# Gated linear attention: the first eight loads re-cut, re-ordered and issued from two engines

## The chip, the cores and the metric

One of the eight cores of a Trainium2 chip runs the whole kernel. The metric is the device time of one execution in microseconds. The kernel before was run three times.

## What is computed

Eight batches of linear attention with eight heads, 576 tokens and 64 channels a head, and behind it a gated block over 512 channels. Cut to what matters:

```
q_s = exp(q - max over the 64 channels);  q_s /= sum over the 64 channels + 1e-9
k_s = exp(k - max over the 576 tokens);   k_s /= sum over the 576 tokens + 1e-9
kv  = einsum('bhsd,bhse->bhde', k_s, v)
x   = einsum('bhsd,bhde->bhse', q_s, kv)          # then heads side by side: 512 channels
gate_pre[s] = sum over 5 taps of conv_w[tap] * x[s - 4 + tap]
gate = 1 / (1 + exp(-gate_pre))
out  = (gate * (x @ w_val)) @ w_out
```

q, k and v are float32. The two weight matrices and the convolution's taps are 64-bit floats; they reach the core as pairs of 32-bit words, and the core makes float32 numbers of them.

## The kernel before, in words

The tokens of a batch lie on the partitions in four chunks of 128 and a tail of 64; the tails of two batches share one tile. For batches 0 and 1 the keys come with the channels on the partitions, as four blocks of 128 channels by 576 tokens; later batches take another way, which the change does not touch.

There is no loop nest that sets the order. `ORDER` (line 32) is a list of some thousand steps written out by hand; the last lines of the kernel call the function of each step in that order. Every engine takes its instructions in this order, one after the other, and waits at the first one whose data are not there. So the place of a step among the others is the kernel's schedule.

The steps at the start that this text speaks of, with their lines:

- `load_q b c0 c1` (206) loads the chunks c0 to c1 of a batch's q; with c1 = 5 on an even batch the tail comes too, as a transfer of its own. `load_kc b p` (314) loads a block of keys, `load_words i` (225) a slab of weight words (0 to 3 of w_val, 4 to 7 of w_out), `load_ident` (233) the identity matrix that TensorE's transposes use. All of them are issued on SyncE (SP). The framework gives each transfer one of eight completion semaphores in turn, and a transfer that takes a semaphore again waits on SP until the transfer that had it before has landed. So at most eight transfers are under way, and SP's queue stands still while it waits.
- A weight slab becomes float32 by `part` (238, ScalarE here), `field` (244), `scaled` (250) and `signed` (254, VectorE, two instructions) and `joined` (260, GpSimd), which needs both sides. `w_high` (269) rounds it into the first of two weight tiles.
- Of q, `q_max` (357, VectorE) takes the negative maximum per head. Chunk 2 of batch 0 goes through `q_each` (381), eight ScalarE exponentials with the maximum as their bias; the other chunks through `q_sub` (363, GpSimd) and `q_exp` (368, ScalarE). `q_sum` (372) and `q_mul` (387) divide by the sum.
- Of a block of keys, `k_top` (318, VectorE) takes the negative maximum and `k_raise` (324, ScalarE) the exponential; `k_turn` (328) transposes on TensorE and `k_turned` (335) copies back.

Line 588 loads the table of the exponential on ScalarE before any step; the four memsets behind it run on GpSimd.

Of the kernel before, what the change touches and what calls it, by code (L numbers as in the profile page):

```python
# [11 lines left out]
AF = mybir.ActivationFunctionType  # L12
# [7 lines left out]
NB = C // P  # L20
# [9 lines left out]


ORDER = [step.strip() for step in """
    load_words 3, load_q 0 2 5, load_kc 0 2, load_kc 0 0, load_q 0 1 2, load_kc 0 3, load_kc 0 1, load_words 0, field 3,
    part 3 a, scaled 3 v, signed 3, joined 3, load_ident, q_max 0 2 3, load_words 1, q_max 0 3 5, q_each 0 2,
    w_high 3 p, load_q 0 0 1, k_top 0 2, q_sub 0 4 p, load_q 1 0 5, k_top 0 0, k_raise 0 2, load_kc 1 3, q_sub 0 3 p,
    q_max 0 1 2, k_raise 0 0, load_kc 1 0, k_top 0 3, q_sub 0 1 p, q_exp 0 4 5, load_v 0, k_top 0 1, k_raise 0 3,
    load_vt 0, part 0 a, field 0, k_turn 0 1, load_words 2, scaled 0 v, q_exp 0 3 4, signed 0, k_raise 0 1, load_kc 1 2,
# [109 lines left out]
def gated_linear_attention(ctx: ExitStack, tc: tile.TileContext, q, k, v, qt, kt, vt, kc, km, w_val, w_out, ident_in, out):  # L147
    nc = tc.nc
# [11 lines left out]
    def block(tag, name, bufs, dtype=F32, n=S):  # L160
        return work.tile([P, S], dtype, tag=tag, name=name, bufs=bufs)[:, :n]

    def pair(name, dtype, tag="pair", bufs=6):
        return work.tile([P, 2 * S], dtype, tag=tag, name=name, bufs=bufs)
# [18 lines left out]
    T = {}  # L183
# [4 lines left out]
    def cols(h):  # L188
        return {"a": slice(0, C), "l": slice(0, C // 2), "r": slice(C // 2, C)}[h]
# [6 lines left out]
    def load_k(b, h="a"):  # L196
        if ("k", b) not in T:
            T["k", b] = big.tile([P, 4, C], F32, tag="k", name=f"k{b}")
        nc.sync.dma_start(out=T["k", b][:, :, cols(h)], in_=k[b, :, :, cols(h)])

    def load_kt(b):
        if b % 2 == 0:
            T["kt", b] = T["kt", b + 1] = big.tile([P, C], F32, tag="kt", name=f"kt{b}", bufs=1)
            nc.sync.dma_start(out=T["kt", b], in_=kt[b // 2])

    def load_q(b, c0=0, c1=5):
        if ("q", b) not in T:
            T["q", b] = big.tile([P, 5, C], F32, tag="q", name=f"q{b}")
        nc.sync.dma_start(out=T["q", b][:, c0:min(c1, 4)], in_=q[b, :, c0:min(c1, 4)])
        if c1 == 5 and b % 2 == 0:  # L210
            nc.sync.dma_start(out=T["q", b][:, 4], in_=qt[b // 2])

    def load_v(b):
        T["v", b] = big.tile([P, 4, H, D + 1], F32, tag="v", name=f"v{b}")
# [7 lines left out]
    def slab(i):  # L222
        return slice(P * (i % NB), P * (i % NB) + P)

    def load_words(i):

        n = C + TAPS * (i < NB)
        place = ("under", 2) if i in (4, 5) else ("pair", 6)
        t = pair(f"words{i}", I32, *place)[:, :2 * n]
        T["words", i] = t.rearrange("p (n t) -> p n t", t=2)  # L230
        nc.sync.dma_start(out=t, in_=(w_val, w_out)[i // NB][i % NB])

    def load_ident():
        nc.sync.dma_start(out=ident, in_=ident_in)

# [73 lines left out]

    def load_kc(b, p):
        t = T["kc", b, p] = block(("gh", "gl")[b], f"kc_{b}_{p}", 4)
        nc.sync.dma_start(out=t, in_=kc[b, p])

    def k_top(b, p):
        if ("ktop", b) not in T:
# [260 lines left out]
    ident = const.tile([P, P], F32, tag="ident", name="ident")  # L580
# [4 lines left out]
    ]  # L585
    kvd = [const.tile([P, NB, P], F32, tag=f"kvd{i}", name=f"kvd{i}") for i in range(2)]
    ktz = [const.tile([P, C], F32, tag=f"ktz{i}", name=f"ktz{i}") for i in range(2)]
    nc.scalar.preload_act_table(AF.Exp)
    for t in kvd + ktz:
        nc.gpsimd.memset(t, 0.0)  # L590

# [51 lines left out]
```

## Time and profile before

| | us |
|---|---|
| three runs | 304.69, 305.14, 306.5 (median 305.14) |
| profiled execution | 305.72 |
| span of its instructions | 303.9 |

| engine | busy us | share of the span |
|---|---|---|
| TensorE (PE) | 279.1 | 92% |
| its weight loads (PEld) | 271.1 | 89% |
| VectorE (DVE) | 255.5 | 84% |
| ScalarE (ACT) | 216.2 | 71% |
| GpSimd (POOL) | 220.4 | 73% |

The profiled execution is 1.8 us longer than the span, which runs from the first instruction to the last; a sum made within the span is carried to the execution's time by adding these 1.8 us. The share of an engine is a mean over the whole span. At the start TensorE has nothing to do yet, and the other engines and the transfers decide; there the timeline (start, duration, engine, line, what is written from what, and in brackets the idle time before it with what ended it) and the chain of waits say more than the shares. SPq stands for SP's queue of transfers: its rows are the issues, not the transfers.

### The profile page before, as it was taken

The numbers are of one execution on the slowest core, as the hardware profiler recorded it, in microseconds if no ns is written. First come the engines' busy times: TensorE is split into PE (matmuls) and PEld (weight loads), VectorE is DVE, ScalarE is ACT, GpSimd is POOL, SyncE is SP. The second block draws the span as 40 slices with busy tenths as digits, with TensorE's granted clock in tenths as the row PEclk, the third lists the DMA queues.
The fourth block names the chain that finished last, engine by engine and source line by source line (L and its number), as shares of the span: only waits on it lengthen the run. The fifth ranks groups of instructions, "written<-read, shape, count | busy, mean of one in ns | idle before, by whom it ended". The sixth has DMA issues, their size and how long they took to land.

```text
span 303.9 us, 6467 instructions
## 1 busy us (share of the span) xinstructions
PE 279.1 (92%) x2536; PEld 271.1 (89%) x2536; DVE 255.5 (84%) x350; ACT 216.2 (71%) x357; POOL 220.4 (73%) x206
## 2 busy tenths in 40 slices
PE   0347899999999899999999999999999999999995
PEld 0336699999989799999999999999998999999995
DVE  3999999999999798999999898999779876836611
ACT  3999999967795996869673964659496885464220
POOL 4677959799989699659787879784886949752500
PEclk9978999999999999999999999999999999999999
DMA  7999491389598822618597099023201210021012
GB/s 240 408 405 396 156 397 45 103 187 361 194 319 261 327 102 75 217 54 284 158 395 304 39 259 332 17 90 106 38 0 39 80 41 0 2 116 41 0 62 96
DMA packets 17454, 51.25 MB, mean 169 GB/s; under 512 B 2705, under 2 KB 3089, under 8 KB 14737
## 3 DMA queue, kind: packets, MB, share of 16 engines
q1 hardware_dynamic: 17424, 50.85, 47.9%
q8 instruction: 20, 0.33, 0.5%
q14 instruction: 10, 0.07, 0.1%
HBM read 41.39 MB, written 9.45 MB: 167 GB/s over the span
## 4 chain that ended last, share of the span: by engine, by line
PE 66%; ACT 11%; DVE 10%; DMA 7%; issue 2%; POOL 2%; SPq 1%; ACTq 0%; DVEq 0%
PE out L534 26%; PE val L534 25%; PE x L487 7%; PE kv L407 4%; PE qTps L439 3%; DVE qs L377 3%; DMA q<-in_q 3%; DMA words<-in_w_val 2%; ACT q L392 2%; DMA out<-o 2%; DVE qm L361 1%; ACT L523 1%; DVE qs L378 1%; ACT qT L171 1%; DVE gate L511 1%
## 5 line engine op out<-in xcount | busy, mean ns | idle before, releaser
L534 PE MATMUL val<-x,w_val_hi 128*128 128x288 f32 x512 | 88.4, 294 | 0.0
L534 PEld LDWEIGHTS val<-x,w_val_hi 128*128 128x128 f32 x512 | 74.8, 188 | 0.0
L511 DVE SCALAR_TENSOR_TENSOR gate<-x,cw,gate 128x573 f32<-128x573 f32 (+3 forms) x91 | 72.1, 807 | 2.2 <-ACT gate L500 1.2
L520 POOL TENSOR_TENSOR gate<-gate,far 128x572 f32<-128x572 f32 (+3 forms) x37 | 49.5, 1341 | 27.3 <-ACT far L516 26.4
L534 PE MATMUL out<-gh,w_out_lo 128*128 128x288 f32 x256 | 55.9, 297 | 1.1 <-ACT o L171 0.6
L534 PE MATMUL val<-x,w_val_lo 128*128 128x288 f32 x256 | 56.0, 299 | 0.0
L534 PE MATMUL out<-gh,w_out_hi 128*128 128x288 f32 x256 | 55.0, 294 | 0.0
L534 PEld LDWEIGHTS out<-gh,w_out_lo 128*128 128x128 f32 x256 | 41.2, 188 | 2.1 <-ACT o L171 0.9
L534 PEld LDWEIGHTS val<-x,w_val_lo 128*128 128x128 f32 x256 | 40.7, 188 | 0.7 <-DVE x L173 0.2
L534 PEld LDWEIGHTS out<-gh,w_out_hi 128*128 128x128 f32 x256 | 41.2, 188 | 0.0
L560 POOL TENSOR_TENSOR gl<-g,gh 128x576 fp32r<-128x576 f32 x24 | 34.6, 1449 | 7.2 <-ACT gh L171 5.0
L534 PE MATMUL out<-gl,w_out_hi 128*128 128x288 f32 x256 | 39.2, 294 | 0.0
L516 ACT ACTIVATE far<-x,cw 128x572 f32<-128x572 f32 (+3 forms) x37 | 27.0, 745 | 13.7 <-DVE gate L511 6.7
L534 PEld LDWEIGHTS out<-gl,w_out_hi 128*128 128x128 f32 x256 | 35.7, 188 | 0.0
L552 DVE TENSOR_TENSOR g<-val,gate 128x576 f32<-128x576 f32 x32 | 24.0, 751 | 10.0 <-PE val L534 5.8
L366 POOL TENSOR_TENSOR q<-q,qm 128x512 f32<-128x512 f32 x29 | 31.0, 1086 | 0.7 <-issue 0.7
L171 ACT COPY o<-out 128x576 f32<-128x576 f32 x27 | 17.2, 637 | 16.7 <-PE out L534 11.5
L301 POOL TENSOR_TENSOR k<-k,kmax 128x512 f32<-128x512 f32 x21 | 28.6, 1377 | 0.1
L506 DVE TENSOR_TENSOR x<-x,x 128x576 fp32r<-128x576 f32 x32 | 23.2, 747 | 6.3 <-ACT far L516 4.1
L523 ACT ACTIVATE gate<-gate 128x576 f32<-128x576 f32 x32 | 21.1, 685 | 8.4 <-DVE gate L511 5.4
L394 POOL TENSOR_TENSOR q<-q,qs 128x512 f32<-128x512 f32 x25 | 26.0, 1048 | 0.8 <-DVE qs L379 0.6
L500 ACT ACTIVATE gate<-x,cw 128x576 f32<-128x576 f32 x27 | 19.9, 747 | 6.8 <-PE x L487 5.2
(88 smaller groups left out, 522.1 us busy)
## 6 DMA issues: line engine op xcount, KB each, us to landing
out<-o SPq DMA_DIRECT2D x31, 288.0 KB, 2.2
v<-in_v SPq DMA_DIRECT2D x8, 1040.0 KB, 8.9
q<-in_q SPq DMA_DIRECT2D x7, 1024.0 KB, 7.7
km<-in_k_strided SPq DMA_DIRECT2D x24, 288.0 KB, 4.8
k<-in_k SPq DMA_DIRECT2D x6, 1024.0 KB, 7.9
kc<-in_k_channels SPq DMA_DIRECT2D x8, 288.0 KB, 7.6
words<-in_w_val SPq DMA_DIRECT2D x4, 517.0 KB, 6.9
words<-in_w_out SPq DMA_DIRECT2D x4, 512.0 KB, 7.7
```

The source lines that it names most:

```text
L301: engine(e).tensor_sub(kk[r, cs], kk[r, cs], mx[r, cs])
L366: engine(e).tensor_tensor(qq, qq, m, op=ALU.add if b < 2 else ALU.subtract)
L394: engine(e).tensor_mul(qq, qq, s.unsqueeze(2).broadcast_to([P, H, D]))
L487: nc.tensor.matmul(T["x", b, p][:, cs], a, z[:, cs], start=(i == 0), stop=(i == len(parts) - 1))
L506: nc.vector.tensor_sub(xl, T["x", b, p], T["xh", b, p].bitcast(F32))
L511: nc.vector.scalar_tensor_tensor(out=a, in0=x, scalar=w, in1=a, op0=ALU.mult, op1=ALU.add)
L516: nc.scalar.activation(T["far", b, p, j], T["x", b, p][:, :S - n], AF.Copy, scale=cw[:, p, j:j + 1])
L520: nc.gpsimd.tensor_add(a, a, T["far", b, p, j])
L523: nc.scalar.activation(T["gate", b, p], T["gate", b, p], AF.Sigmoid)
L534: nc.tensor.matmul(ps[:, cs], a[:, kb, ms], z[:, cs], start=(i == 0), stop=(i == len(parts) - 1))
L552: nc.vector.tensor_mul(T["g", b, m], T["val", b, m], T["gate", b, m])
L560: engine(e).tensor_sub(T["gl", b, m], T["g", b, m], T["gh", b, m].bitcast(F32))
```

## The change

It touches the first rows of `ORDER` and the functions behind them.

- q of batch 0 was loaded as chunks 2 and 3 in one transfer of 512 KB and the tail as a second; now chunk 2 alone (256 KB) is the first transfer of SP, then chunk 3, then the tail.
- Weight slab 3 (517 KB), the first transfer before, and key block 2 of batch 0 (288 KB) are issued by ScalarE.
- The table of the exponential is loaded by a step of its own, `table`, behind these two issues on ScalarE.
- `q_max 0 2 3` and `q_each 0 2` stand ahead of weight slab 3's steps; `q_max 0 3 5` keeps its place behind them.

```diff
 ORDER = [step.strip() for step in """
-    load_words 3, load_q 0 2 5, load_kc 0 2, load_kc 0 0, load_q 0 1 2, load_kc 0 3, load_kc 0 1, load_words 0, field 3,
-    part 3 a, scaled 3 v, signed 3, joined 3, load_ident, q_max 0 2 3, load_words 1, q_max 0 3 5, q_each 0 2,
+    load_q 0 2 3, load_words 3 a, load_q 0 3 5, load_kc 0 2 a, table, load_kc 0 0, load_q 0 1 2, load_kc 0 3, load_kc 0 1,
+    load_words 0, q_max 0 2 3, q_each 0 2, field 3, part 3 a, scaled 3 v, signed 3, joined 3, load_ident, load_words 1, q_max 0 3 5,
     w_high 3 p, load_q 0 0 1, k_top 0 2, q_sub 0 4 p, load_q 1 0 5, k_top 0 0, k_raise 0 2, load_kc 1 3, q_sub 0 3 p,
...
+    def queue(e):
+        return {"s": nc.sync, "a": nc.scalar}[e]
+
+    def table():
+        nc.scalar.preload_act_table(AF.Exp)
+
...
-    def load_q(b, c0=0, c1=5):
+    def load_q(b, c0=0, c1=5, e="s"):
...
-        nc.sync.dma_start(out=T["q", b][:, c0:min(c1, 4)], in_=q[b, :, c0:min(c1, 4)])
+        queue(e).dma_start(out=T["q", b][:, c0:min(c1, 4)], in_=q[b, :, c0:min(c1, 4)])
...
-        nc.sync.dma_start(out=t, in_=(w_val, w_out)[i // NB][i % NB])
+        queue(e).dma_start(out=t, in_=(w_val, w_out)[i // NB][i % NB])
...
-        nc.sync.dma_start(out=t, in_=kc[b, p])
+        queue(e).dma_start(out=t, in_=kc[b, p])
...
-    nc.scalar.preload_act_table(AF.Exp)
```

How the order moves is shown for three engines. A row has the line, the instruction, what is written from what (words3 is weight slab 3, kc_0_2 key block 2 of batch 0, q0 and qm_0 batch 0's q and its maxima, ktop_0 the maxima of the keys, e3 and f3 the two halves of a slab under work; the last number is a buffer's) and in brackets the semaphores that it waits for; DMAHW0 to DMAHW7 are the eight of the transfers.

SP's queue at the start of the program, before:

```order
L231 DMA words3_89<-in_w_val 128x1034
L209 DMA q0_91<-in_q 128x1024
L211 DMA q0_91<-in_q_tail 128x512
L316 DMA kc_0_2_94<-in_k_channels 128x576
L316 DMA kc_0_0_96<-in_k_channels 128x576
L209 DMA q0_91<-in_q 128x512
L316 DMA kc_0_3_99<-in_k_channels 128x576
L316 DMA kc_0_1_101<-in_k_channels 128x576
L231 DMA words0_103<-in_w_val 128x1034 [waits DMAHW0_49]
L234 DMA ident_72<-in_ident 128x128 [waits DMAHW1_49]
```

And with the change:

```order
L215 DMA q0_88<-in_q 128x512 x2
L217 DMA q0_88<-in_q_tail 128x512
L322 DMA kc_0_0_97<-in_k_channels 128x576
L215 DMA q0_88<-in_q 128x512
L322 DMA kc_0_3_100<-in_k_channels 128x576
L322 DMA kc_0_1_102<-in_k_channels 128x576 [waits DMAHW0_49]
L237 DMA words0_104<-in_w_val 128x1034 [waits DMAHW1_49]
L240 DMA ident_72<-in_ident 128x128 [waits DMAHW2_49]
```

Two rows have left SP, and one transfer has become two. There are now nine transfers ahead of weight slab 0, so key block 1 is the first that waits for a semaphore (that of slab 3, DMAHW0); slab 0 waits for q's chunk 2 (DMAHW1) where it waited for slab 3.

ScalarE at the start, before:

```order
L588 ACT_TABLE_LOAD
L177 ACTIVATE f3_107<-words3_89 128x517 [waits DMAHW0_49]
L385 ACTIVATE q0_91<-q0_91,qm_0_114 128x64 [waits DMAHW1_49,DVE_49]
L385 ACTIVATE q0_91<-q0_91,qm_0_114 128x64 x7
L326 ACTIVATE kc_0_2_94<-kc_0_2_94,ktop_0_129 128x576 [waits DMAHW3_49,DVE_49]
```

And with the change:

```order
L237 DMA words3_90<-in_w_val 128x1034
L322 DMA kc_0_2_94<-in_k_channels 128x576
L205 ACT_TABLE_LOAD
L391 ACTIVATE q0_88<-q0_88,qm_0_106 128x64 [waits DMAHW1_49,DVE_49]
L391 ACTIVATE q0_88<-q0_88,qm_0_106 128x64 x7
L177 ACTIVATE f3_118<-words3_90 128x517 [waits DMAHW0_49]
L332 ACTIVATE kc_0_2_94<-kc_0_2_94,ktop_0_130 128x576 [waits DMAHW2_49,DVE_49]
```

Two issues stand ahead of the table's load, and the eight exponentials of chunk 2 have passed ahead of slab 3's `part`.

VectorE at the start, before:

```order
L248 TENSOR_SCALAR e3_105<-words3_89 128x517 [waits DMAHW0_49]
L181 TENSOR_SCALAR e3_105<-e3_105 128x517 [waits DVE_49]
L257 TENSOR_SCALAR e3_105<-e3_105 128x517 [waits DVE_49]
L258 SCALAR_TENSOR_TENSOR e3_105<-words3_89,e3_105 128x517 [waits DVE_49]
L361 TENSOR_REDUCE qm_0_114<-q0_91 128x8 [waits DMAHW1_49]
L361 TENSOR_REDUCE qm_0_114<-q0_91 128x16 [waits DMAHW2_49]
```

And with the change:

```order
L367 TENSOR_REDUCE qm_0_106<-q0_88 128x8 [waits DMAHW1_49]
L254 TENSOR_SCALAR e3_116<-words3_90 128x517 [waits DMAHW0_49]
L181 TENSOR_SCALAR e3_116<-e3_116 128x517 [waits DVE_49]
L263 TENSOR_SCALAR e3_116<-e3_116 128x517 [waits DVE_49]
L264 SCALAR_TENSOR_TENSOR e3_116<-words3_90,e3_116 128x517 [waits DVE_49]
L367 TENSOR_REDUCE qm_0_106<-q0_88 128x16 [waits DMAHW4_49,DMAHW3_49]
```

The maximum of chunk 2 has moved from the fifth place to the first. All that follows on VectorE, and all of GpSimd's and TensorE's rows, keep their order.

More of the change, by code (lines that the diff above doesn't have):

```diff
@@ L204, in load_kt @@
             nc.sync.dma_start(out=T["kt", b], in_=kt[b // 2])
-    def load_q(b, c0=0, c1=5):
+    def load_q(b, c0=0, c1=5, e="s"):
         if ("q", b) not in T:
             T["q", b] = big.tile([P, 5, C], F32, tag="q", name=f"q{b}")
-        nc.sync.dma_start(out=T["q", b][:, c0:min(c1, 4)], in_=q[b, :, c0:min(c1, 4)])
+        queue(e).dma_start(out=T["q", b][:, c0:min(c1, 4)], in_=q[b, :, c0:min(c1, 4)])
         if c1 == 5 and b % 2 == 0:
-            nc.sync.dma_start(out=T["q", b][:, 4], in_=qt[b // 2])
+            queue(e).dma_start(out=T["q", b][:, 4], in_=qt[b // 2])
     def load_v(b):
@@ L223, in slab, with load_words @@
         return slice(P * (i % NB), P * (i % NB) + P)
-    def load_words(i):
+    def load_words(i, e="s"):
         n = C + TAPS * (i < NB)
@@ L230, in load_words, with load_ident @@
         T["words", i] = t.rearrange("p (n t) -> p n t", t=2)
-        nc.sync.dma_start(out=t, in_=(w_val, w_out)[i // NB][i % NB])
-    def load_ident():
-        nc.sync.dma_start(out=ident, in_=ident_in)
+        queue(e).dma_start(out=t, in_=(w_val, w_out)[i // NB][i % NB])
+    def load_ident(e="s"):
+        queue(e).dma_start(out=ident, in_=ident_in)
     def part(i, e="a"):
@@ L309, in kt_exp, with load_kc @@
         nc.scalar.activation(ktz[b % 2][r, cs], T["kt", b][r, cs], AF.Exp)
-    def load_kc(b, p):
+    def load_kc(b, p, e="s"):
         t = T["kc", b, p] = block(("gh", "gl")[b], f"kc_{b}_{p}", 4)
-        nc.sync.dma_start(out=t, in_=kc[b, p])
+        queue(e).dma_start(out=t, in_=kc[b, p])
     def k_top(b, p):
```

## The prediction

> **What bounds the kernel now.** I read the chain of waits first, because it tells which stretch the change can reach. Its columns are start, duration and what the end of the kernel hung on.
>
> ```profile
> 4.90 7.30 DMA words<-in_w_val
> 12.20 0.02 issue
> 12.23 0.44 DVE e L248
> ...
> 27.38 0.62 DVE ktop L322
> 28.00 0.02 issue
> 28.03 0.77 ACT kc L326
> 28.80 1.21 ACT qT L171 x2
> 30.01 0.04 issue
> 30.06 1.24 PE x L487 x4
> ```
>
> The start hangs on one transfer, weight slab 0, which lands at 12.20. Then VectorE works without a break to 28.00, ScalarE to 30.06, and from there the chain is mostly TensorE (66% of the span in the page's shares). The change acts ahead of 12.23 only; what it wins or loses there reaches the end only if VectorE and ScalarE carry it to 30.06. So I read the busy times by stretch next (busy time and count of each engine, then TensorE's granted clock, the transfer engines' busy share and GB/s).
>
> ```profile
> 0.00:12.20 12.20, 0.00 (x0) 0.00 (x0) 7.10 (x11) 6.60 (x14) 7.00 (x13) 1.00 0.86 304
> 12.20:28.00 15.80, 10.65 (x115) 9.56 (x116) 15.43 (x27) 15.12 (x39) 11.74 (x13) 0.78 1.03 403
> 1.66:5.07 3.41, 0.00 (x0) 0.00 (x0) 0.65 (x2) 1.03 (x2) 0.98 (x3) 1.00 0.94 269
> 5.07:8.48 3.41, 0.00 (x0) 0.00 (x0) 3.27 (x6) 1.31 (x6) 1.78 (x2) 1.00 1.00 371
> ```
>
> From 12.20 to 28.00 VectorE is busy 15.43 of 15.80 us and ScalarE 15.12: both are full, and the rest is ScalarE's wait for VectorE shown below. Ahead of it VectorE is busy 7.10 us and mostly waits for its first data. The transfer engines are busy from early on but move 269 and then 371 GB/s, against 403 later. VectorE's timeline has these waits in brackets:
>
> ```profile
> 4.38 0.43 DVE L248 TENSOR_SCALAR e<-words 128x517 f32<-128x517 f32 x1 [4.38 <-DMA words<-in_w_val]
> ...
> 6.45 1.98 DVE L361 TENSOR_REDUCE qm<-q 128x8 f32<-128x512 f32 x2
> 8.35 1.40 DVE L322 TENSOR_REDUCE ktop<-kc 128x1 f32<-128x576 f32 x2
> 9.67 0.68 DVE L361 TENSOR_REDUCE qm<-q 128x8 f32<-128x512 f32 x1
> 10.26 1.40 DVE L322 TENSOR_REDUCE ktop<-kc 128x1 f32<-128x576 f32 x2
> ...
> 12.23 0.43 DVE L248 TENSOR_SCALAR e<-words 128x517 f32<-128x517 f32 x1 [0.56 <-DMA words<-in_w_val]
> ```
>
> It starts at 4.38, when slab 3 has landed, works to 11.66 (10.26 + 1.40) and stands 0.56 us until slab 0 is there. So two things set 12.23: VectorE's queue, with 0.56 us to spare, and the landing of slab 0. A gain needs both.
>
> **The change, part by part.** When do the first two transfers land now? SP's rows before (issue, duration), its wait, and one small transfer from later on:
>
> ```profile
> 0.74 0.38 SPq L231 DMA_DIRECT2D words<-in_w_val  x1
> ...
> 4.90 0.47 SPq L231 DMA_DIRECT2D words<-in_w_val  x1
> 6.45 0.33 SPq L234 DMA_DIRECT2D ident<-in_ident  x1
> ...
> SPq L234 <- DMA q<-in_q: 1.1, 1, 1.1
> ...
> km<-in_k_strided SPq DMA_DIRECT2D x1, 288.0 KB, 2.8
> ```
>
> Slab 3's 517 KB, issued at 0.74, were there at 4.38. The identity's issue waited for q's chunks 2 and 3, so these 512 KB landed by 6.45: 2.07 us behind, 253 GB/s. With the change chunk 2 (256 KB) and slab 3 are issued side by side at about 0.74.
>
> - Chunk 2's landing, L2. Lower bound: had it the engines for itself, the km row's 2.8 us for 288 KB gives 0.74 + 2.8 = 3.5. Upper bound: both land together, after 773 KB at the old rate, 4.38 + 2.07 / 2 = 5.4. I take equal shares by bytes: chunk 2 is there when about 512 KB have come, 4.4.
> - Slab 3's landing, L3: from 4.4 (unchanged) to 5.4 (behind all 773 KB). I take 5.0, 5.4 less the gain of the next point.
> - Slab 0's landing. The bytes ahead of it are the same; only the slow ramp can shrink, by a gain g. Lower bound 0: the transfer engines' share is already 0.94 in the stretch from 1.66. Upper bound: at 403 GB/s the 512 KB would take 1.30 us in place of 2.07 (0.77 won); the km row leaves 2.8 - 0.73 = 2.07 us for what doesn't move bytes, and slab 3's bytes need 1.31 at 403, so 3.38 in place of 3.64 (0.26 won). Together 1.0. I take 0.4, nearer to 0 because of the 0.94: slab 0 can be used at 12.23 - 0.40 = 11.83.
>
> VectorE. Its work ahead of slab 0 is the same 7.28 us (4.38 to 11.66), of which chunk 2's maximum is 0.68, the like of the row at 9.67. Now the maximum goes first: its queue is through at the later of L2 + 0.02 + 7.28 = 11.70 and L3 + 0.02 + 6.60 = 11.62. That is ahead of 11.83, so slab 0 decides: -0.40. The cover is 0.13 us; the bounds of L2 and L3 give 11.0 to 12.7.
>
> ScalarE and GpSimd. Chunk 2's exponentials, now ahead of slab 3's `part`, hold up GpSimd's `joined`, and what it does for q:
>
> ```profile
> 0.73 1.28 ACT L588 ACT_TABLE_LOAD   x1 [0.73 <-PEq L632]
> 4.38 0.68 ACT L177 ACTIVATE f<-words 128x517 int32<-128x517 uint32 x1 [2.37 <-DMA words<-in_w_val]
> 7.17 2.02 ACT L385 ACTIVATE q<-q,qm 128x64 f32<-128x64 f32 x8 [2.11 <-DVE qm L361]
> 9.13 1.44 ACT L326 ACTIVATE kc<-kc,ktop 128x576 f32<-128x576 f32 x2
> 10.47 0.61 ACT L370 ACTIVATE q<-q 128x512 f32<-128x512 f32 x1
> 11.04 0.78 ACT L326 ACTIVATE kc<-kc,ktop 128x576 f32<-128x576 f32 x1
> 12.23 0.69 ACT L177 ACTIVATE f<-words 128x517 int32<-128x517 uint32 x1 [0.41 <-DMA words<-in_w_val]
> ...
> 6.64 1.28 POOL L261 TENSOR_TENSOR f<-e,f 128x517 int32<-128x517 int32 x1 [4.00 <-DVE e L258]
> 7.98 0.61 POOL L173 CAST w_val_hi<-f 128x512 fp32r<-128x512 f32 x1
> 8.55 3.04 POOL L366 TENSOR_TENSOR q<-q,qm 128x512 f32<-128x512 f32 x3
> ```
>
> From L2: the maximum 0.72 with its hops, the eight exponentials 1.96 (7.17 to 9.13), `part` 0.68, a hop of 0.1, `joined` 1.34 (6.64 to 7.98), the cast 0.57 (7.98 to 8.55), the first subtraction 1.04 (3.04 is three, overlapping), its exponential 0.6, a key block 0.65 to 0.7, so 7.66 us to slab 0's `part`, the row at 12.23. With L2 = 4.4 that is 12.06, behind slab 0 (11.83) but ahead of the old 12.23. ScalarE is then 0.23 us later than VectorE would like, and has this to spare:
>
> ```profile
> ACT kc L326 <- DVE ktop L322: 0.7, 1, 0.7
> ```
>
> 0.7 us of waiting for VectorE just ahead of 28.03. So the delay on ScalarE costs nothing; without that cover it would cost 0.23. The table's load (1.28) moves behind two issues of at most 0.5 each and ends by 3.0, while ScalarE waits for chunk 2's maximum until about 5.1; uncovered, at most 1.28. SP has one issue fewer, but key block 1 now waits for slab 3 and slab 0's issue moves from 4.90 to about 5.5. It took 7.30 us from issue to landing there, most of it in the queue, so 0.6 us later costs nothing; if the queue ran dry it would be 0.6. GpSimd, 1.3 us later up to 12.8, is ready before slab 0's `joined` needs it (14.47 less 0.4). Each later transfer still waits for the one eight places ahead, so all landings move with the ramp.
>
> The sum: -0.40 at 12.23, carried by VectorE's queue to 28.00 and by ScalarE to TensorE's start, 29.66 in place of 30.06; from there nothing is changed. The profiled 305.72 becomes 305.3; it stands 0.58 above the median of the runs, so against 305.14 I forecast 304.7.
>
> **The rivals.**
>
> *The ramp doesn't shrink* (0.27): g = 0, slab 0 lands at 12.20 as before, and VectorE's head start only lengthens its 0.56 us wait: 305.1. For it speaks the share of 0.94; against it that these busy engines moved 269 GB/s, time in which a second queue may get bytes through. The Trainium skill ("DMA: Bandwidth & Descriptors", "Issuing engines are not separate DMA queues") says that transfers started by different engines run on the same 16 DMA engines and interleave, and that issuing from several only saves the sequencer's time; by that rule this rival is the result. No run here yet has a second queue.
>
> *The full ramp* (0.17): chunk 2 by 3.5, slab 3 by 4.4, g = 1.0. VectorE is through at 11.0, ScalarE at 11.2, slab 0 usable at 11.23: -1.0, so 304.1. Against it: the first bytes cost more than 2 us whatever the queue.
>
> *The first data come later* (0.11, the slower side): L2 = L3 = 5.4. VectorE is through at 12.7, +0.5, and ScalarE at 13.1, +0.85, of which its 0.7 us cover all but 0.15: VectorE decides, 305.6. It decides from L2 = 4.93 on (4.93 + 0.02 + 7.28 = 12.23), only 0.5 above what I take.
>
> *ScalarE's queue is served behind SP's* (0.03): slab 3 would come behind the six transfers that SP has issued by 3.5, with the last key blocks, near 10.1 (they are used from 10.26 on): 10.1 + 6.6 = 16.7, +4.5, 309.6. Nothing in a trace with one queue excludes it.
>
> *The clock* (0.04). The rows of five stretches:
>
> ```profile
> 15.31:18.72 3.41, 0.93 (x8) 0.69 (x7) 3.34 (x6) 3.41 (x8) 3.27 (x4) 1.00 1.03 409
> ...
> 22.14:25.55 3.41, 3.41 (x69) 3.41 (x67) 3.34 (x8) 3.41 (x10) 3.06 (x4) 0.50 1.06 418
> 25.55:28.96 3.41, 2.24 (x25) 1.63 (x22) 3.27 (x8) 2.73 (x7) 3.07 (x4) 1.00 0.99 381
> 28.96:32.38 3.42, 2.88 (x20) 2.38 (x21) 3.34 (x7) 3.42 (x6) 1.34 (x2) 1.00 0.71 287
> 32.38:35.79 3.41, 3.18 (x19) 2.25 (x16) 3.34 (x7) 3.36 (x6) 3.41 (x5) 1.00 0.11 30
> ```
>
> After a stretch with 0.93 us of TensorE work the granted clock fell to 0.50; after 2.24 of 3.41 it stayed at 1.00. Were it to fall at 28.96, TensorE's 2.88 us, on the chain by then, would take as long again, less 0.5 idle: +2.3; with the next stretch (3.18 less 0.2) +5.3, 310.4. A shift of 0.4 us changes 2.24 by a fraction of that, far from 0.93. The Trainium skill ("TensorE: Matmul & The Clock Gate", "Part 1") has the window run freely, so it may lie otherwise in each run; the trace agrees, its clock changes fit the 3.41 us stretches above.
>
> **How the numbers follow.** My forecast has 0.38 with its own range of 304.4 to 304.9; the rest as given. About 1%, 3 us, is what a measurement here can tell from no change. None of the first four cases reaches that; the served-behind case and half of the clock's do: slower 0.05. Faster by 3 us would need three times the full ramp: 0.03, for what I don't see. The same: 0.92. The range goes from the full ramp to the later start, each widened by 0.3 for the spread of the runs (304.69 to 306.5): 303.8 to 305.9.
>
> **What would show it.** In the changed profile VectorE's first row should be chunk 2's maximum near 4.4, slab 3's first row near 5.1, slab 0's near 11.8 with a wait for the transfer of 0.1 to 0.2 us, ScalarE's slab 0 row near 12.1 without one, and TensorE's first row of line 487's matmul (now 493) near 29.7. I am wrong if slab 0 is used at 12.2 or later, if the wait ahead of it is not for the transfer, or if the gain at 12 has gone by 30.

## The result and the profile after

| | before | changed |
|---|---|---|
| median, us | 304.79 (12 runs, 304.08 to 306.5) | 306.93 (12 runs, 306.27 to 307.9) |
| profiled execution, us | 305.72 | 306.78 |
| its span, us | 303.9 | 304.9 |

The changed kernel takes 1.0070 times as long as before (95% interval 1.0051 to 1.0090), about 2.1 us more. That is still within 1%, but the sign is the other one and the time lies above the range of 303.8 to 305.9.

The chain of waits of the changed kernel, from its first piece (start, duration, what the end hung on):

```profile
0.73 5.40 DMA q<-in_q
...
6.16 0.69 DVE qm L367
...
29.14 0.62 DVE ktop L328
...
29.79 0.78 ACT kc L332
```

The start hung on slab 0, at 12.20. Now it hangs on q's chunk 2, the transfer that was cut small and put first: it lands at 6.13, and VectorE works from there to 29.76 without a break. `k_raise`, at 28.03 before, starts at 29.79: +1.76. TensorE's first matmul of line 493 (487 before) starts at 31.82 where it was 30.06, and its fourth group, with which the chain comes to TensorE now, at 38.16 where it was 36.40: +1.76 both times. So the loss is made ahead of slab 1 and carried.

VectorE's timeline of the changed kernel up to slab 1's first row:

```profile
6.16 0.69 DVE L367 TENSOR_REDUCE qm<-q 128x8 f32<-128x512 f32 x1 [6.16 <-DMA q<-in_q]
6.76 0.42 DVE L254 TENSOR_SCALAR e<-words 128x517 f32<-128x517 f32 x1
7.21 0.43 DVE L181 TENSOR_SCALAR e<-e 128x517 f32<-128x517 f32 x1
...
11.88 1.40 DVE L328 TENSOR_REDUCE ktop<-kc 128x1 f32<-128x576 f32 x2
13.20 0.57 DVE L254 TENSOR_SCALAR e<-words 128x517 f32<-128x517 f32 x1
13.80 1.15 DVE L181 TENSOR_SCALAR e<-e 128x517 f32<-128x517 f32 x1
...
16.07 0.43 DVE L254 TENSOR_SCALAR e<-words 128x517 f32<-128x517 f32 x1
```

Two losses stand in it. Slab 0's first row is at 13.20 in place of 12.23 (+0.97), and there is no bracket at it: VectorE comes late from its own queue. From there to slab 1's first row (16.07) it takes 2.87 us; before, that row was at 14.24, 2.01 us behind (+0.86). The rows at 7.21 and 13.80 are the same instruction on tiles of the same shape, 0.43 and 1.15 us. GpSimd's and ScalarE's rows of that time tell what lies beside it:

```profile
9.53 1.27 POOL L267 TENSOR_TENSOR f<-e,f 128x517 int32<-128x517 int32 x1 [6.89 <-ACT f L177]
10.87 0.61 POOL L173 CAST w_val_hi<-f 128x512 fp32r<-128x512 f32 x1
11.44 3.23 POOL L372 TENSOR_TENSOR q<-q,qm 128x512 f32<-128x512 f32 x3
```

```profile
1.65 1.28 ACT L205 ACT_TABLE_LOAD   x1 [1.65 <-PEq L637]
6.88 2.02 ACT L391 ACTIVATE q<-q,qm 128x64 f32<-128x64 f32 x8 [3.95 <-DVE qm L367]
8.80 0.65 ACT L177 ACTIVATE f<-words 128x517 int32<-128x517 uint32 x1
13.71 0.67 ACT L177 ACTIVATE f<-words 128x517 int32<-128x517 uint32 x1
```

The three subtractions, at 8.55 before, run from 11.44 to 14.67, over VectorE's rows of slab 0. They waited for `joined` (9.53), that for ScalarE's `part` (8.80), and that for the eight exponentials, which now stand ahead of it (6.88).

Busy times by stretch of the changed kernel (TensorE, its weight loads, VectorE, ScalarE, GpSimd, then TensorE's granted clock, the transfer engines' share and GB/s):

```profile
1.66:5.07 3.41, 0.00 (x0) 0.00 (x0) 0.00 (x0) 1.27 (x1) 0.98 (x3) 1.00 0.84 195
5.07:8.48 3.41, 0.00 (x0) 0.00 (x0) 2.22 (x5) 1.60 (x7) 0.00 (x0) 1.00 1.02 391
```

In the first stretch the transfers move 195 GB/s, where it was 269: the slow beginning, which I thought could only shrink, has grown. SP's queue shows the landings of what was issued in it:

```profile
3.68 3.14 SPq L322 DMA_DIRECT2D kc<-in_k_channels  x2
6.86 0.45 SPq L237 DMA_DIRECT2D words<-in_w_val  x1
...
13.02 0.33 SPq L226 DMA_DIRECT2D vt<-in_v_tail  x1
```

Key block 1 (the second of the two issues at 3.68) waits for slab 3, so slab 3 was there by about 6.5; the issue of v's tail, here as before, waits for slab 0, which landed at 13.00 (12.20 before).

The profiled executions differ by only 1.06 us, the medians by 2.1. The place is the small `krow` transfer, behind which the issue of `kmax` waits. SP's queue in the changed kernel, and then before:

```profile
87.75 0.33 SPq L297 DMA_DIRECT2D krow<-kpk  x1
92.24 0.33 SPq L302 DMA_DIRECT2D kmax<-krow  x1
```

```profile
85.94 0.33 SPq L291 DMA_DIRECT2D krow<-kpk  x1
91.28 0.33 SPq L296 DMA_DIRECT2D kmax<-krow  x1
```

The changed kernel comes 1.81 us late to the first and 0.96 late to the second, since the transfer took 4.5 us here and 5.3 in before's profile. Over the profiles of this study it took 3.9 to 5.7. The profiled execution of before lies 0.9 us above its median; in this pair 0.85 us of the lateness went there, and the medians tell more than the pair. One run of the experiments below (309.62 us, with GpSimd busy) was in a second, slower state, and the time and ratio given leave it out.

### The profile page after: what moved, and what is told of

It reads as the page before. It is cut to its first block, busy times and chain, and to the rows that moved or that the text cites. A ratio compares the mean times of both kernels' runs of the same rounds, so it can differ in the third digit from the quotient of the medians.

```text
span 304.9 us, 6471 instructions
## 1 busy us (share of the span) xinstructions
PE 280.9 (92%) x2536; PEld 272.8 (89%) x2536; DVE 256.8 (84%) x350; ACT 216.0 (71%) x357; POOL 220.6 (72%) x206
## 4 chain that ended last, share of the span: by engine, by line
PE 67%; ACT 14%; DVE 13%; DMA 3%; issue 1%; POOL 0%; ACTq 0%
PE out L540 27%; PE val L540 25%; PE x L493 6%; PE kv L413 5%; DVE qs L383 3%; PE qTps L445 3%; DVE qm L367 2%; ACT q L398 2%; DMA q<-in_q 2%; ACT qT L171 2%; DVE ktop L328 2%; DMA out<-o 2%; ACT q L376 1%; DVE qs L384 1%; DVE gate L517 1%
## 5 line engine op out<-in xcount | busy, mean ns | idle before, releaser
L367 DVE TENSOR_REDUCE qm<-q 128x8 f32<-128x512 f32 (+3 forms) x12 | 20.7, 1735 | 6.2 <-DMA q<-in_q 6.2
```

Source lines behind the costliest of these rows:

```text
L367: nc.vector.tensor_reduce(out=T["qm", b][:, cs], in_=qq, axis=AX.X, op=ALU.max, negate=b < 2)
```

## The experiments

Three suspects were to be parted: the smaller first pieces, the second queue, and the new order of the work. Where nothing else is said, the row of slab 0 is VectorE's first row of that slab, and the lateness is read at slab 1's first row, against 14.24 before. Each kernel was measured beside further runs of the kernel before (medians 305.37 us for the first four experiments, 305.11 for `joined` later and the second run of the three chunks, 305.32 for the others). The ratio with its 95% interval is estimated from the single runs; it is not the quotient of the two medians.

**One queue.** The changed kernel, all issues on SP again.

```diff
-    load_q 0 2 3, load_words 3 a, load_q 0 3 5, load_kc 0 2 a, table, load_kc 0 0, load_q 0 1 2, load_kc 0 3, load_kc 0 1,
+    load_q 0 2 3, load_words 3, load_q 0 3 5, load_kc 0 2, table, load_kc 0 0, load_q 0 1 2, load_kc 0 3, load_kc 0 1,
```

> The changed kernel with both of ScalarE's transfers back on SP, at the same places of the list (chunk 2, slab 3, chunk 3, tail, key block 2, ...); the order of the work stays the changed one. Theory: the second queue is at fault; the two queues' packets take turns, so neither first transfer gets ahead, and the slow ramp is spent on both. Then here chunk 2 lands alone by 3.3 to 3.7, slab 3 by about 5.2, slab 0 at 12.2 again (13.0 with two queues), VectorE's slab 0 rows start near 12.2 and keep their 2.0 us, and the time is 304.3 to 305.0, the old one or a little less. Rival: the smaller pieces (more and shorter packets in the slow ramp) are at fault; then slab 0 lands near 13.0 here too and the time stays at 306.5 to 307.

Measured: 305.73 us, 1.0024 (1.0005 to 1.0043). VectorE's rows:

```profile
4.97 0.69 DVE L367 TENSOR_REDUCE qm<-q 128x8 f32<-128x512 f32 x1 [4.97 <-DMA q<-in_q]
...
13.10 0.65 DVE L254 TENSOR_SCALAR e<-words 128x517 f32<-128x517 f32 x1 [0.38 <-DMA words<-in_w_val]
...
15.33 0.43 DVE L254 TENSOR_SCALAR e<-words 128x517 f32<-128x517 f32 x1
```

Chunk 2 comes at 4.94 in place of 6.13, but slab 0 as late as with two queues (13.07 and 13.00). So the second queue does not lengthen the slow beginning, as I had thought after the result; the pieces do. Neither answer came out as a whole: even alone in front chunk 2 is later than the 3.7 that I expected, and later than slab 3 before with twice its bytes (4.36), and the time lies between the two that I gave. What the second queue does is to hold back the first transfer by 1.2 us, and through the later GpSimd work VectorE's rows of slab 0: the lateness is 1.09 us here and 1.83 with it.

**Slab 3 alone on ScalarE.** The kernel before with this one transfer moved (the `table` step stands behind it, q's transfers are whole again, the order of the work is the old one).

```diff
-    load_words 3, load_q 0 2 5, load_kc 0 2, load_kc 0 0, load_q 0 1 2, load_kc 0 3, load_kc 0 1, load_words 0, field 3,
-    part 3 a, scaled 3 v, signed 3, joined 3, load_ident, q_max 0 2 3, load_words 1, q_max 0 3 5, q_each 0 2,
+    load_words 3 a, load_q 0 2 5, load_kc 0 2, table, load_kc 0 0, load_q 0 1 2, load_kc 0 3, load_kc 0 1,
+    load_words 0, field 3, part 3 a, scaled 3 v, signed 3, joined 3, load_ident, q_max 0 2 3, load_words 1, q_max 0 3 5, q_each 0 2,
```

> The kernel before with one edit: weight slab 3 is issued by ScalarE, the table's load behind it. Old cut, old order of work. Theory (second queue): slab 3 and q's chunks 2 and 3 take turns and land together near 6.3 in place of 4.36 and 6.43; VectorE starts at 6.3 and reaches slab 0 at 6.3 + 7.28 = 13.6; slab 0 lands at 12.2 if only the sharing counts, near 12.8 if the second queue also lengthens the ramp. Time 306.0 to 306.5. Rival (small pieces at fault, the queue harmless): slab 3 at 4.4 to 4.7, time 304.8 to 305.1.

Measured: 307.01 us, 1.0062 (1.0035 to 1.0089). VectorE's first row and that of slab 0, then SP's issue behind slab 0's landing:

```profile
6.47 0.43 DVE L254 TENSOR_SCALAR e<-words 128x517 f32<-128x517 f32 x1 [6.47 <-DMA words<-in_w_val]
...
13.44 0.52 DVE L254 TENSOR_SCALAR e<-words 128x517 f32<-128x517 f32 x1
```

```profile
12.17 0.33 SPq L226 DMA_DIRECT2D vt<-in_v_tail  x1
```

Slab 0 lands as before (12.15), though SP issues it only at 6.47, for 4.90: so the late issue, which the changed kernel has too (6.86), does not delay it by itself. But slab 3 (6.45) and q's chunks (6.14) land nearly together, where they landed at 4.36 and 6.43, one behind the other, before: the two queues take turns, and what VectorE waits for first comes about when the second would. Its 7 us of work from there on end at 13.44. By the times, one row moved to a second queue costs about as much as the whole change; by the lateness, 1.31 of its 1.83 us.

**The old order of work.** The changed kernel with its loads, and the steps behind them as before.

```diff
-    load_words 0, q_max 0 2 3, q_each 0 2, field 3, part 3 a, scaled 3 v, signed 3, joined 3, load_ident, load_words 1, q_max 0 3 5,
+    load_words 0, field 3, part 3 a, scaled 3 v, signed 3, joined 3, load_ident, q_max 0 2 3, load_words 1, q_max 0 3 5, q_each 0 2,
```

> The changed kernel's loads with the old order of the work: slab 3's steps ahead of chunk 2's maximum and exponentials. The loads land as in the changed kernel (slab 3 near 6.5, slab 0 near 13.0). VectorE starts at 6.5 and reaches slab 0 at 6.5 + 7.28 = 13.75 in place of 13.2; GpSimd's slab 3 step comes at 8.7 in place of 9.5. Theory (the stretching of slab 0's rows from 2.0 to 2.9 us is GpSimd's three subtractions running into them): GpSimd is through by 13.8, slab 0's rows take 2.0 to 2.2 us again and end near 15.8 to 15.9 in place of 16.07; time 306.5 to 306.9. Rival (the stretch comes from the late loads or something else that this keeps): the rows take 2.9 us and end at 16.6, time 307.3 or more.

Measured: 306.77 us, 1.0052 (1.0034 to 1.0070). VectorE starts at 6.47, reaches slab 0 at 13.45 and slab 1 at 15.55: its rows of slab 0 take 2.1 us again. GpSimd's subtractions run earlier:

```profile
10.64 3.04 POOL L372 TENSOR_TENSOR q<-q,qm 128x512 f32<-128x512 f32 x3
```

They end at 13.68, when slab 0's first row is nearly done. The lateness is 1.31 us; the new order costs VectorE the other 0.5. The difference of the two times (306.77 and 306.93) is too small to show it.

**GpSimd busy, nothing else changed.** The kernel before with two idle additions behind the subtractions, so that GpSimd is at work while VectorE does slab 0 (the added function reads and writes a tile that nobody uses; one more memset at the start fills it).

```diff
-    q_max 0 1 2, k_raise 0 0, load_kc 1 0, k_top 0 3, q_sub 0 1 p, q_exp 0 4 5, load_v 0, k_top 0 1, k_raise 0 3,
+    q_max 0 1 2, k_raise 0 0, load_kc 1 0, k_top 0 3, q_sub 0 1 p, spare, spare, q_exp 0 4 5, load_v 0, k_top 0 1, k_raise 0 3,
...
+    def spare():
+        nc.gpsimd.tensor_add(idle, idle, idle)
```

> The kernel before with two additions on a spare 128x512 tile given to GpSimd behind its third subtraction (GpSimd is idle there from 11.6 to 14.5), and one more memset at the start; nothing waits for them. They should run from 11.6 to 13.7. Theory: GpSimd's two-input operation and VectorE's tensor_scalar on the same memory exclude each other, so slab 0's rows on VectorE (12.23 to 14.24, 2.0 us) stretch by 0.6 to 1.0 us, and as VectorE is full to 28 the whole kernel is later by that: 305.4 to 305.8. Rival: the two don't disturb one another; rows and time unchanged, 304.8.

Measured: 305.51 us, 1.0031 (1.0007 to 1.0055). GpSimd's added rows, and VectorE's of slab 0 and slab 1:

```profile
11.54 2.22 POOL L202 TENSOR_TENSOR idle<-idle 128x512 f32<-128x512 f32 x2
```

```profile
12.21 0.66 DVE L251 TENSOR_SCALAR e<-words 128x517 f32<-128x517 f32 x1 [0.58 <-DMA words<-in_w_val]
12.90 1.15 DVE L181 TENSOR_SCALAR e<-e 128x517 f32<-128x517 f32 x1
...
15.17 0.43 DVE L251 TENSOR_SCALAR e<-words 128x517 f32<-128x517 f32 x1
```

The loads are those of before, slab 0 is used at 12.21, and still slab 0's rows take 2.96 us: 0.66 and 1.15 where 0.43 each is usual. The collision alone makes the 0.9 us. The Trainium skill ("SBUF — State Buffer", "Who interferes with whom") says that VectorE in a mode with two ports, which `tensor_scalar` can enter, shares a port pair with GpSimd and one of the two then blocks for the other's whole instruction, and that `tensor_reduce` never contends. The traces agree: in the changed kernel the two maxima of the keys at 11.88, beside the subtractions, keep their 1.40 us.

**Small pieces alone.** The kernel before, with q's chunks 2 and 3 as two transfers.

```diff
-    load_words 3, load_q 0 2 5, load_kc 0 2, load_kc 0 0, load_q 0 1 2, load_kc 0 3, load_kc 0 1, load_words 0, field 3,
+    load_words 3, load_q 0 2 3, load_q 0 3 5, load_kc 0 2, load_kc 0 0, load_q 0 1 2, load_kc 0 3, load_kc 0 1, load_words 0, field 3,
```

> The kernel before with one edit: q's chunks 2 and 3 come as two transfers of 256 KB in place of one of 512 KB; slab 3 still first, all on SP, old order of the work. Theory (in the slow ramp packets count, not bytes: in all traces so far about 255 packets have started by 5.5 us, whatever their size): the second 128 packets carry 256 KB less, slab 3 lands at 4.4 as before, slab 0 at 12.7 to 13.0, time +0.4 to +0.7. Rival (the ramp depends on bytes or on what comes first): slab 0 at 12.2, time unchanged.

Measured: 306.77 us, 1.0046 (1.0022 to 1.0070). VectorE's rows that wait for a transfer:

```profile
4.29 0.43 DVE L248 TENSOR_SCALAR e<-words 128x517 f32<-128x517 f32 x1 [4.29 <-DMA words<-in_w_val]
...
6.56 0.69 DVE L361 TENSOR_REDUCE qm<-q 128x8 f32<-128x512 f32 x1 [0.17 <-DMA q<-in_q]
8.97 1.22 DVE L361 TENSOR_REDUCE qm<-q 128x16 f32<-128x1024 f32 x1 [1.72 <-DMA q<-in_q_tail]
...
13.90 0.43 DVE L248 TENSOR_SCALAR e<-words 128x517 f32<-128x517 f32 x1 [0.48 <-DMA words<-in_w_val]
```

Slab 3 is unhurt. But chunk 2 alone lands at 6.54, when both chunks were there before (6.43); chunk 3 follows at 8.16, and slab 0 at 13.88, a microsecond beyond what I expected of it; the time is 1.4 us longer, where I expected 0.4 to 0.7. Cutting a transfer in two gave the first half no sooner and the rest later.

How much later is less sure. The trace notes sixteen completions for each transfer, and the landing is the last of them. In this profile one falls behind: of chunk 3 fifteen are there by 7.23, of slab 0 by 12.93. Against before (12.11 and 12.20) slab 0's fifteenth completion is 0.82 us later and its last 1.68, and the profiled execution (307.72) lies 0.95 above the median of its runs. So what the cut costs in every execution is not settled by this one profile.

**Larger pieces.** The opposite: the kernel before, with chunks 1 to 3 as one transfer of 768 KB.

```diff
-    load_words 3, load_q 0 2 5, load_kc 0 2, load_kc 0 0, load_q 0 1 2, load_kc 0 3, load_kc 0 1, load_words 0, field 3,
+    load_words 3, load_q 0 1 5, load_kc 0 2, load_kc 0 0, load_kc 0 3, load_kc 0 1, load_words 0, field 3,
```

> The kernel before with one edit the other way: q's chunks 1, 2 and 3 come as one transfer of 768 KB (6 KB a packet), and the transfer of chunk 1 behind the key blocks is left out. Same bytes ahead of slab 0. Theory (packets count): the ramp brings 256 KB more, slab 3 at 4.4, the three chunks at 6.4 to 6.8, slab 0 at 11.5 to 11.8; VectorE is through at 11.7 and starts slab 0 by 11.8 in place of 12.23: time -0.3 to -0.5. Rival (bytes count): the chunks land at 7.0 to 7.2, slab 0 at 12.2; VectorE waits 0.6 us for chunk 2 and the time is +0.1 to +0.3.

> The same kernel as three_chunks, once more, because its interval held no change. VectorE was 0.64 us earlier from slab 0 on in its profile. Theory (VectorE's queue carries this to the end): -0.4 to -0.7, ratio 0.9977 to 0.9987. Rival (it is lost further on): ratio 0.9995 or more.

Measured: 304.82 us, 0.9989 (0.9968 to 1.0009), and once more 304.93, 0.9983 (0.9962 to 1.0004). VectorE's rows of the first:

```profile
4.42 0.43 DVE L248 TENSOR_SCALAR e<-words 128x517 f32<-128x517 f32 x1 [4.42 <-DMA words<-in_w_val]
6.54 1.91 DVE L361 TENSOR_REDUCE qm<-q 128x8 f32<-128x512 f32 x2
...
11.59 0.43 DVE L248 TENSOR_SCALAR e<-words 128x517 f32<-128x517 f32 x1
```

Slab 0 is used 0.64 us earlier, VectorE has no gap ahead of it, and the lateness is -0.64 and, in the second profile, -0.49 us. In the first profile this lead is lost further on, as the rival had it: 0.47 us in a wait for batch 1's q,

```profile
17.25 1.22 DVE L361 TENSOR_REDUCE qm<-q 128x16 f32<-128x1024 f32 x1 [0.47 <-DMA q<-in_q]
```

and more at 78.89, where a `tensor_scalar` row beside GpSimd takes 2.06 us for 1.31 before; `krow` is issued 0.79 us late. In the second profile it is still 0.42 early. The two medians are 0.5 and 0.2 us below that of before, each with an interval that still holds no change: the earlier slab 0 is shown in the rows, a faster kernel is not.

What the transfers carried between 1.5 and 5.5 us stands in the line of sums of the transfer view. In before:

```profile
DMA packets 275, 1.03 MB, mean 258 GB/s; under 512 B 20, under 2 KB 20, under 8 KB 275
```

In the changed kernel:

```profile
DMA packets 300, 0.82 MB, mean 204 GB/s; under 512 B 25, under 2 KB 25, under 8 KB 300
```

With the small pieces alone:

```profile
DMA packets 330, 0.89 MB, mean 222 GB/s; under 512 B 26, under 2 KB 26, under 8 KB 330
```

With the three chunks in one transfer:

```profile
DMA packets 260, 1.24 MB, mean 311 GB/s; under 512 B 16, under 2 KB 16, under 8 KB 260
```

In the beginning these four kernels move 260 to 330 packets of 2.7 to 4.8 KB in the mean (the bytes by the packets). A piece of one chunk comes in smaller packets than one of two or three, and among these four the beginning carries more bytes the larger its packets are. The expectation's 255 were, without the packets under 512 B, 238 to 282 in the traces made until then. The other kernels do not all fit: slab 3 on ScalarE has 245 packets of 4.0 KB and 0.98 MB, and the two experiments that follow have 383 of 2.6 KB (0.98 MB) and 372 of 3.3 KB (1.22 MB). The cut also changes how many transfers stand ahead of slab 0, nine for eight and seven with the three chunks. The next experiment has nine too.

**Many tiny packets first.** Does every packet cost the same there? The kernel before with the identity (128 packets of 512 bytes) as the first transfer.

```diff
-    load_words 3, load_q 0 2 5, load_kc 0 2, load_kc 0 0, load_q 0 1 2, load_kc 0 3, load_kc 0 1, load_words 0, field 3,
-    part 3 a, scaled 3 v, signed 3, joined 3, load_ident, q_max 0 2 3, load_words 1, q_max 0 3 5, q_each 0 2,
+    load_ident, load_words 3, load_q 0 2 5, load_kc 0 2, load_kc 0 0, load_q 0 1 2, load_kc 0 3, load_kc 0 1, load_words 0, field 3,
+    part 3 a, scaled 3 v, signed 3, joined 3, q_max 0 2 3, load_words 1, q_max 0 3 5, q_each 0 2,
```

> The kernel before with the identity matrix (64 KB, 128 packets of 512 bytes) as the first transfer, ahead of slab 3. Theory (packets count): these 128 packets use up the first half of the ramp; slab 3 lands near 6 in place of 4.36, slab 0 at 13.0 to 13.4, time +0.8 to +1.3. Rival (bytes or time count): 64 KB cost 0.2 us, slab 3 at 4.6, slab 0 at 12.2 to 12.4, time +0.0 to +0.2.

Measured: 305.55 us, 1.0011 (0.9993 to 1.0029). VectorE's first row:

```profile
5.13 0.43 DVE L248 TENSOR_SCALAR e<-words 128x517 f32<-128x517 f32 x1 [5.13 <-DMA words<-in_w_val]
```

Slab 3 is there at 5.11, 0.75 us later, for 64 KB that are 0.16 us of the later 400 GB/s; were packets all that counts it would have been near 6. Slab 0 lands at 12.57, between the two answers as well. So in this run 128 small packets cost more than their bytes would, and less than if every packet cost the same: the strict form of the idea fell. And one more transfer ahead of slab 0, which is no piece of another, delays it by 0.37 us, less than the cut (0.80 and more); packet size and number are not parted further.

**A pause between the issues.** Is it the time since the start, or the issues that follow one another closely? The kernel before, with two memsets of key block 2's tile ahead of its load, which SP must wait for.

```diff
     def load_kc(b, p):
...
+        if (b, p) == (0, 2):
+            for _ in range(2):
+                nc.gpsimd.memset(t, 0.0)
```

> The kernel before with two memsets of key block 2's tile on GpSimd (behind its four first memsets) ahead of that block's load, so that SP issues three transfers by 2.1 and stands still until 3.7 to 4.0. One look. Theory A (the ramp is slow because SP is issuing further transfers then): from 2.1 to 3.8 packets run at their later speed, slab 3 lands at 3.8 to 4.1, and the slow packets move to 4 to 6 us. Theory B (a cold start, whatever SP does): slab 3 at 4.3 to 4.4, q's chunks at 6.4, as before.

Measured, in a single run: 304.76 us. The stretches from 1.66:

```profile
1.66:5.07 3.41, 0.00 (x0) 0.00 (x0) 0.69 (x2) 1.03 (x2) 2.07 (x5) 1.00 0.95 313
5.07:8.48 3.41, 0.00 (x0) 0.00 (x0) 3.34 (x6) 1.41 (x6) 1.82 (x2) 1.00 0.99 303
```

Before, these were 269 and 371. SP stood still until 3.82, and q's chunks landed at 5.67 in place of 6.43; then the slow time came later, and slab 0 landed at 13.07 in place of 12.20. Neither answer came out as put down: slab 3 came as in B (4.32), q's chunks did not. The slow time isn't tied to the start alone, and it came some 3 us behind the resumed issues, not with them. What makes it stays open.

**`joined` later.** The changed kernel, with the GpSimd work that holds up the subtractions moved behind them.

```diff
-    load_words 0, q_max 0 2 3, q_each 0 2, field 3, part 3 a, scaled 3 v, signed 3, joined 3, load_ident, load_words 1, q_max 0 3 5,
-    w_high 3 p, load_q 0 0 1, k_top 0 2, q_sub 0 4 p, load_q 1 0 5, k_top 0 0, k_raise 0 2, load_kc 1 3, q_sub 0 3 p,
+    load_words 0, q_max 0 2 3, q_each 0 2, field 3, part 3 a, scaled 3 v, signed 3, load_ident, load_words 1, q_max 0 3 5,
+    load_q 0 0 1, k_top 0 2, q_sub 0 4 p, load_q 1 0 5, k_top 0 0, k_raise 0 2, load_kc 1 3, q_sub 0 3 p,
...
-    load_v 2, q_mul 0 4 p, q_each 0 0, k_top 1 3, q_sub 1 1 p, tail_turn 0, q_max 1 2 4, q_mul 0 2 p, q_each 1 0,
+    load_v 2, q_mul 0 4 p, q_each 0 0, k_top 1 3, q_sub 1 1 p, tail_turn 0, q_max 1 2 4, q_mul 0 2 p, joined 3, w_high 3 p, q_each 1 0,
```

> The changed kernel with slab 3's two steps on GpSimd (joined 3, w_high 3) moved from ahead of the three subtractions of q to GpSimd's idle place near 21 us. The loads land as in the changed kernel. Theory (of the 1.83 us that VectorE is late behind slab 0's rows, 0.97 come from the late first data and 0.86 from the subtractions, late by 1.3 us, running into slab 0's rows): the subtractions run from 10.1 to 13.1, slab 0's rows start near 13.2, take 2.0 us again in place of 2.9 and end near 15.2; time +0.8 to +1.2 over the kernel before in place of +2.1. Rival (the collision only moves time that VectorE loses anyway, or joined 3 near 21 us delays the later steps by as much): rows shorter but the time still +1.7 to +2.3.

Measured: 307.72 us, 1.0079 (1.0051 to 1.0106). The subtractions run at 10.18 to 13.22, and slab 0's rows take 2.0 us again (13.25 to 15.25). But the moved work meets VectorE elsewhere, GpSimd's row first:

```profile
21.88 1.28 POOL L267 TENSOR_TENSOR f<-e,f 128x517 int32<-128x517 int32 x1
```

```profile
22.17 1.28 DVE L263 TENSOR_SCALAR e<-e 128x517 int32<-128x517 int32 x1
23.48 0.99 DVE L264 SCALAR_TENSOR_TENSOR e<-words,e 128x517 int32<-128x517 int32 x1
```

These two take 0.43 and 0.70 us where GpSimd is idle. VectorE's row of line 384 that stood at 26.25 before comes at 28.59, +2.34, where the changed kernel has it at 28.00, +1.75. The collision was moved, not removed, and the time (2.6 us above the 305.11 beside it) lies beyond both answers.

**The lateness and the time.** VectorE's lateness at slab 1's first row, over the time before, against the measured ratio:

| kernel | lateness, us | that over 305 us | ratio less 1 (95%) |
|---|---|---|---|
| changed | 1.83 | 0.60% | 0.70% (0.51 to 0.90) |
| small pieces alone | 1.68 | 0.55% | 0.46% (0.22 to 0.70) |
| slab 3 on ScalarE | 1.31 | 0.43% | 0.62% (0.35 to 0.89) |
| old order of work | 1.31 | 0.43% | 0.52% (0.34 to 0.70) |
| one queue | 1.09 | 0.36% | 0.24% (0.05 to 0.43) |
| GpSimd busy | 0.93 | 0.30% | 0.31% (0.07 to 0.55) |
| identity first | 0.37 | 0.12% | 0.11% (-0.07 to 0.29) |
| three chunks | -0.64 | -0.21% | -0.11% (-0.32 to 0.09) |
| three chunks again | -0.49 | -0.16% | -0.17% (-0.38 to 0.04) |

Every interval holds what the lateness gives. (The kernel with `joined` later loses behind that row; its 2.34 us at line 384 are 0.77%, for 0.79% measured.) The intervals are wide, though, and the medians alone would put the one-queue kernel at 0.12% and the busy GpSimd at 0.05%: for the small losses the rows are the evidence. The pause has one run and no interval. It does not fit by itself: its row of slab 1 is 0.87 us late (15.11), and its 304.76 us are 0.56 below the median beside it. In that profile it is 0.82 late up to `krow`, which then takes 3.9 us for 5.3.

## Why the prediction was wrong

- **Chunk 2's landing (4.4, bounds 3.5 to 5.4; measured 6.13) failed.** What failed is "equal shares by bytes". Slab 3 has twice the bytes and came only 0.34 us behind chunk 2 (6.47 and 6.13). Each is 128 packets, of 4.1 and of 2 KB; between 2.5 and 4.5 us 67 and 84 of them start in the trace's packet records, so the two queues take turns nearer to packet by packet than byte by byte, and the smaller transfer gets hardly a lead by its size. The price was wrong too: the upper bound took both transfers' 773 KB at the rate of before, but the beginning with the smaller pieces is slower, 195 GB/s for 269. Slab 3 alone on ScalarE shows the first part, the one-queue kernel and the small pieces alone the second.
- **Slab 0's landing ("the bytes ahead of it are the same; only the slow ramp can shrink", bounds 0 to 1.0; measured +0.80) failed in its sign.** The bytes were the same and the packets were not. That nothing excluded a loss was a gap in the argument: the bound of 0 rested on the busy share of 0.94, which fell to 0.84. The later issue of slab 0, put at nothing, was right: it came at 6.86 and not 5.5, but the kernel with slab 3 alone on ScalarE has it at 6.47 and lands it at 12.15.
- **VectorE's queue** behaved as written: from the later start it works 7.0 us without a gap and decides over slab 0, which could have been used at 13.02. The rival "the first data come later", put at 0.11, named this course; with the measured landing its rule gives 6.13 + 0.02 + 7.28 = 13.43, for 13.20 measured. Its 305.6 was too small because its landing of 5.4 was, and because it knew nothing of the next point.
- **GpSimd ("1.3 us later up to 12.8, is ready before slab 0's `joined` needs it") failed.** I asked who waits for GpSimd, and not what runs beside it. It came 2.9 us later (11.44 for 8.55), of which the later landing makes 1.7, and cost VectorE 0.86 us with nobody waiting for it. The busy GpSimd alone shows that. The warning stood in before's trace, in a row that I did not look at: a `tensor_scalar` row of line 378 (128x16) at 26.25 took 0.85 us beside GpSimd's multiplications of 23.97 to 27.06, and one at 32.32, beside no more than a small copy, 0.17.
- **ScalarE** was right: 7.66 us from chunk 2's landing to slab 0's `part` give 13.79, measured 13.71. The table's load (1.65 to 2.93) was hidden, as written.
- **The carry** to 28 us on VectorE and to TensorE was right: 1.83 us at 16.07 are 1.76 at TensorE's first matmul of line 493 (31.82, forecast 29.7).
- **The rivals.** The rule of the Trainium skill ("DMA: Bandwidth & Descriptors", "Issuing engines are not separate DMA queues") held as far as it goes: slab 3 on ScalarE moved 244 GB/s between 1.5 and 5.5 us, before 258, so the second queue brought no bandwidth. I took from it that nothing changes; interleaving, which it names too, is what took the lead from the first transfer. ScalarE's queue was not served behind SP's. The clock did what its rival asked for: granted were 0.50 and 0.61 (the third number from the right) in the two stretches that had 1.00 before.

```profile
25.55:28.96 3.41, 2.47 (x32) 1.88 (x29) 3.34 (x7) 3.27 (x11) 3.26 (x5) 0.50 0.97 354
28.96:32.38 3.42, 3.42 (x15) 3.04 (x16) 3.30 (x9) 2.60 (x5) 1.41 (x2) 0.61 0.95 382
```

But the 2.3 us that I put on it did not come. From 29.79 to 38.12 the chain runs over ScalarE, not over TensorE, and the 1.76 us went through unchanged.

So three parts make the loss: the smaller pieces (slab 0 later by 0.8, shown by the one-queue kernel), the second queue (both first transfers near 6.3, shown by slab 3 on ScalarE), and the collision that both, with the new order, bring about. They don't add up one by one, since VectorE waits for the last of them only.

## What to carry to other kernels

At the start of this kernel it paid to let the transfer that the first engine needs go ahead alone in one queue, and not to cut it small; a second queue made the first two arrive together, at the time of the later one. When a step comes later, look not only at who waits for it but at what it will now run beside: here GpSimd work cost VectorE's `tensor_scalar` rows up to 0.85 us each without any wait in the trace. Read such a loss from the same row on both timelines and follow it along the queue; in the nine rows of the table the measured interval holds that lateness, but a profile can lose or win it again further on.

## What the hardware showed that I had not expected

- Between 1.5 and 5.5 us the transfers move 202 to 311 GB/s over all kernels here, later stretches about 400. In the changed kernel, before and with the three chunks they carry 0.82, 1.03 and 1.24 MB in that time, in packets of 2.7, 3.8 and 4.8 KB in the mean.
- Two first transfers of 128 packets each, issued by two engines, land within 0.34 us of each other, whether they have 256 and 517 KB or 512 and 517 KB.
- With a pause between the issues the slow time moves (313, then 303 GB/s, for 269 and 371). Its cause is open.
- A `tensor_scalar` of 128x517 takes 0.43 us alone and up to 1.28 beside a GpSimd instruction; one of 128x16 takes 0.17 and 0.85.
